# Fused sliding-window attention and gated MLP: first attention reordered with fewer fillers, zero fills and a value cast on GpSimd, second tile's attention later

## The chip, the cores and the metric

The kernel runs on one core of one Trainium2 chip. The metric is device time in microseconds (us), from repeated executions. Engine names in the profile: PE is TensorE (PEld its weight loads), DVE is VectorE, ACT is ScalarE, POOL is GpSimd, SP is SyncE. The clock is the share of its full speed that TensorE was granted.

## The reference

Attention over 8 batches of 8 heads, 576 positions, head size 64; heads 0 to 3 see the last 32 positions ("plain"), heads 4 to 7 every fourth of the last 128 ("dilated"). Its output is the input of a gated MLP.

```python
mask_plain = (rel >= 0) & (rel < 32)
mask_dil   = (rel >= 0) & (rel < 32 * 4) & (rel % 4 == 0)
scores = where(masks, (q @ k.T) / 8, -1e9)
attn   = softmax(scores) @ v                    # 8 x 8 x 576 x 64
x = attn.transpose(0, 2, 1, 3).reshape(4608, 512)
h = x @ w_in                                    # 4608 x 2048
g = h * sigmoid(beta * h)
out = g @ w_out                                 # 4608 x 512
```

## The kernel before

The 4608 tokens go through the MLP in nine tiles of 512. The attention of one batch is a list of short steps, and these are dealt out between the up-projection products ("slots") of the tile before. So in the first tile's MLP runs the second attention, in the second tile's MLP the third, and so on. Only the first attention runs with nothing to lie beside, and fillers keep TensorE running there. I call the fill of the pipeline up to the first tanh the start, and the stretch between the first tanh of a tile and that of the next the length of the tile.

In the lists, the first digit of a score, value or output step is the head pair: 0 and 1 are plain, 2 and 3 dilated.

```python
# W<n> n filler matmuls on a zero tile    K<x> Q<x> transposes of keys, queries, and their copies
# S<x><j> scores and exponential          V<x><j> value product and normalisation
# X<x><j> transposes of the output        H<n> first half of an up projection
# v0 v1 v2 casts of values (dilated, dilated, plain)   z0-z2 zero fills   q0-q3 query spreads
FIRST = (
    "W10 K2 W2 Q2 W2 K3 S20 S21 Q3 W2 S22 S23 S30 W1 S31 S32 W1 S33 v0 z0 W3 V20 V21 v1 W3 K0 W2 V22 K1 W3 V23 Q0 W2 "
    "V30 W2 V31 W2 X20 S00 V32 S01 V33 X21 S02 S10 X30 S11 V00 S12 X31 V01 H0 X00 V10 H1 X01 V11 X10 X11 "
    "z1 z2"
).split()
# ... SECOND cut
THIRD = (
    "S20 S21 S22 q0 S23 V20 S30 q1 V21 S31 q2 V22 S32 q3 V23 S33 V30 X20 S00 V31 "
    "S01 X21 V32 S02 V33 v2 S10 V00 X30 S11 V01 S12 X31 V10 X00 V11 X01 X10 X11"
).split()
# ... cut
    FROM = {1: 2}      # tile index 1 (the second): attention steps start at slot 2
# ... cut: the gate of one up-projection product; hps is its PSUM tile
        nc.scalar.activation(
            out=tnh[:], in_=hps, func=ACT.Tanh, scale=beta_half[:, fb:fb + 1])
        nc.vector.scalar_tensor_tensor(
            out=g[:], in0=tnh[:], scalar=1.0, in1=hps, op0=ALU.add, op1=ALU.mult)
# ... cut: a query spread of the third attention, on VectorE
        copy_on(eng)(
            out=qq[b % 2][64 * hf:64 * hf + 64, :, :, e],
            in_=raw[b, "q"][64 * e:64 * e + 64].rearrange("p (h i u) -> p h i u", h=4, i=NI))
# ... cut: who runs the steps that aren't matmuls
            eng = (nc.scalar if name[0] == "v" and (b, name) in ((2, "v2"),) else
                   nc.vector)
```

The tile `hps` lies in PSUM, the memory that this kernel's matmuls write. It is free for the next projection only when the gate product on VectorE has read it. Everything that stands before a gate product in VectorE's queue can so make TensorE wait.

The softmax here doesn't subtract the row's maximum and nothing guards it: scores larger than these inputs give would overflow.

## Time and profile before

| | before |
|---|---|
| median of 3 runs | 329.09 us (328.75 to 329.39) |
| span of the profiled execution | 327.5 us |
| first tanh of tiles 1, 2, 3 | 26.64, 63.38, 96.46 us |
| length of tile 1, 2, 3 | 36.74, 33.08, 30.15 us |
| TensorE clock, every stretch | 1.00 |

A line of the timeline has its start, its duration, the engine and the line of the kernel, the operation with output and input, and in brackets how long the engine was idle just before and what ended that. A line of the waits has the engine and line, what it waited for, the total, how often, and the longest.

### The profile page before, as it was taken

Reading aid. Unit: us, or ns where it says so; the run is one execution under the profiler, and the core shown is the slowest. Engines: PE = TensorE matmul, PEld = TensorE weight load, DVE = VectorE, ACT = ScalarE, POOL = GpSimd, SP = SyncE. Lnnn points to the kernel's source line nnn. Section 1 sums busy time; section 2 is a strip of 40 time slices with the busy share of each in tenths; the row PEclk is TensorE's granted clock in tenths of the full one; section 3 lists DMA queues with packets and bytes.
Section 4 is the critical chain, followed back from the end, with each engine's and each line's share of the span. In section 5 each row is a group of like instructions: output and inputs, shape, how many; then the busy total and the mean of one; then the engine's idle time right before and its main releaser. Section 6 shows DMA issues by size and latency. Waiting matters only on the chain.

```text
span 327.5 us, 6356 instructions
## 1 busy us (share of the span) xinstructions
PE 314.7 (96%) x2395; PEld 168.7 (52%) x2440; DVE 192.4 (59%) x432; ACT 195.6 (60%) x378; POOL 133.1 (41%) x174
## 2 busy tenths in 40 slices
PE   8999999998899999999999999999999999999995
PEld 3664565554555555555555555555555444444444
DVE  4668664787638883967396739673865344244400
ACT  3677774676666766666667666766666555355411
POOL 8943398362376266435643564355434000000000
PEclk9999999999999999999999999999999999999999
DMA  6999999999989798896869778872101210011131
GB/s 90 167 204 197 203 213 162 178 211 224 173 154 178 158 135 167 168 180 90 179 137 187 104 150 177 178 102 66 32 3 32 66 33 33 32 34 32 32 98 65
DMA packets 72223, 41.12 MB, mean 126 GB/s; under 512 B 55024, under 2 KB 67328, under 8 KB 71808
## 3 DMA queue, kind: packets, MB, share of 16 engines
q1 hardware_dynamic: 57264, 25.58, 41.7%
q0 software_dynamic: 14928, 15.14, 29.5%
q8 instruction: 19, 0.31, 0.4%
q14 instruction: 12, 0.10, 0.1%
HBM read 39.32 MB, written 16.52 MB: 170 GB/s over the span
## 4 chain that ended last, share of the span: by engine, by line
PE 90%; DVE 5%; ACT 3%; issue 2%; DVEq 0%; ACTq 0%
PE h_ps L514 32%; PE o_ps L552 28%; PE at L552 5%; PE at L452 4%; PE at L514 4%; PE o_ps L491 3%; PE at L469 3%; PE at L426 2%; PE at L419 2%; DVE g L524 2%; DVE xs L459 1%; ACT tnh L521 1%; PE at L571 1%; PE at L407 1%; PE at L355 1%
## 5 line engine op out<-in xcount | busy, mean ns | idle before, releaser
L524 DVE SCALAR_TENSOR_TENSOR g<-tnh,h_ps 128x512 bf16<-128x512 bf16 x130 | 88.9, 684 | 89.1 <-ACT tnh L521 88.4
L514 PE MATMUL h_ps<-xT,w_in_bf 128*128 128x512 bf16 x503 | 129.4, 379 | 3.0 <-DVE g L524 1.6
L521 ACT ACTIVATE tnh<-h_ps,beta_half 128x512 bf16<-128x512 f32 x130 | 89.4, 687 | 55.9 <-PE h_ps L514 53.3
L552 PE MATMUL o_ps<-w_out_bf,g 128*128 128x512 bf16 x443 | 113.6, 379 | 1.1
L514 PEld LDWEIGHTS <-w_in_bf 128*128 128x128 bf16 x576 | 51.7, 97 | 51.0 <-issue 2.9
L552 PEld LDWEIGHTS <-g 128*128 128x128 bf16 x560 | 50.4, 98 | 47.5
L432 ACT ACTIVATE pt<-at 128x384 bf16<-128x384 f32 (+2 forms) x107 | 46.1, 438 | 15.1 <-PE at L419 7.2
L434 POOL TENSOR_TENSOR pt<-pt,mask_d 96x384 bf16<-96x384 bf16 (+1 forms) x48 | 37.0, 781 | 41.0 <-ACT pt L432 40.3
L459 DVE TENSOR_TENSOR xs<-at,rcp 48x256 bf16<-48x256 f32 (+2 forms) x91 | 42.1, 463 | 8.5 <-PE at L469 4.3
L434 POOL TENSOR_TENSOR pt<-pt,mask_PP 128x384 bf16<-128x384 bf16 x24 | 22.7, 945 | 37.2 <-ACT pt L432 37.1
L452 PEld LDWEIGHTS <-pt 128*128 128x128 bf16 (+2 forms) x448 | 24.5, 97 | 15.8 <-issue 1.0
L560 ACT ACTIVATE osb<-o_ps 128x512 f32<-128x512 f32 x28 | 16.7, 597 | 19.0 <-PE o_ps L552 18.7
L455 DVE RECIPROCAL rcp<-at 48x4 f32<-48x4 f32 (+2 forms) x91 | 16.0, 176 | 7.1 <-PE at L452 6.3
L469 PEld LDWEIGHTS <-xs 96*128 96x128 bf16 (+1 forms) x224 | 13.5, 96 | 11.5 <-issue 2.6
L552 PE MATMUL at<-w_out_bf,g 128*128 128x512 bf16 x79 | 19.3, 379 | 0.1
L426 PEld LDWEIGHTS <-kdT 128*96 128x96 bf16 (+1 forms) x128 | 14.3, 120 | 9.8
L469 PE MATMUL at<-ident_b,xs 96*128 96x96 bf16 (+1 forms) x224 | 18.2, 199 | 0.7 <-ACT xT L475 0.5
L434 POOL TENSOR_TENSOR pt<-pt,mask_FP 128x384 bf16<-128x384 bf16 x12 | 10.9, 911 | 18.5 <-ACT pt L432 18.5
L452 PE MATMUL at<-vd,pt 96*128 96x65 bf16 (+1 forms) x244 | 17.4, 193 | 0.3 <-ACT qq L391 0.3
L426 PE MATMUL at<-qzd,kdT 128*80 128x96 bf16 (+1 forms) x122 | 17.1, 226 | 0.1
L483 ACT COPY xT<-at 128x384 bf16<-128x384 bf16 (+1 forms) x32 | 12.7, 396 | 4.9 <-PE at L469 4.9
L514 PE MATMUL at<-xT,w_in_bf 128*128 128x512 bf16 x54 | 13.6, 379 | 0.2
(116 smaller groups left out, 253.1 us busy)
## 6 DMA issues: line engine op xcount, KB each, us to landing
vp_st<-in_v_dram SPq DMA_DIRECT2D x12, 384.0 KB, 8.8
qk<-in_k_dram POOLq DMA_DIRECT2D x6, 576.0 KB, 6.6
qk<-in_q_dram POOLq DMA_DIRECT2D x6, 576.0 KB, 9.1
vd_st<-in_v_dram SPq DMA_DIRECT2D x6, 384.0 KB, 5.5
w_out_bf<-in_moe_w_out_dram POOLq DMA_DIRECT2D x4, 512.0 KB, 17.1
vd_st<-in_v_dram SPq DMA_DIRECT2D x6, 320.0 KB, 6.6
out_dram<-osb SPq DMA_DIRECT2D x7, 256.0 KB, 2.9
out_dram<-osb SPq DMA_DIRECT2D x8, 224.0 KB, 2.4
```

The source lines that it names most:

```text
L426: nc.tensor.matmul(sc[0:K, a, 0:2 * n], lhsT=kd[b][:, rp, h4, DO[hf]:DO[hf] + K], rhs=qzd[b % 2][:, :, rp, h4, hf * DQ[0]:hf * DQ[0] + n], ...
L432: nc.scalar.activation(out=w, in_=sc[0:K, :, 0:2 * n], func=ACT.Exp, scale=SCALE)
L434: nc.gpsimd.tensor_tensor(out=w, in0=w, in1=mask[0:K], op=ALU.mult)
L452: nc.tensor.matmul(pv[:, a, h2, :], lhsT=pt[x][0:K, c:c + P], rhs=rhs, start=True, stop=True)
L455: nc.vector.reciprocal(out=rcp[0:n, 0:m], in_=pv[0:n, :, :, D])
L459: nc.vector.tensor_tensor(out=xs_t[b, x, jx][:, a0:a0 + m], in0=pv[0:n, :, :, 0:D], in1=rcp[0:n, 0:m].unsqueeze(3).to_broadcast([n, m, 2, ...
L469: nc.tensor.transpose(xp[:, a * n:(a + 1) * n], xs[:, a].rearrange("p h d -> p (h d)"), ident_b[0:n, 0:n])
L514: nc.tensor.matmul(hps, lhsT=w_in_bf[:, kt, fb * P:(fb + 1) * P], rhs=xT[:, kt, t * NTOK:(t + 1) * NTOK], start=(kt == 2), stop=(kt == 1))
L521: nc.scalar.activation(out=tnh[:], in_=hps, func=ACT.Tanh, scale=beta_half[:, fb:fb + 1])
L524: nc.vector.scalar_tensor_tensor(out=g[:], in0=tnh[:], scalar=1.0, in1=hps, op0=ALU.add, op1=ALU.mult)
L552: nc.tensor.matmul(ops[:], lhsT=g_t[t, fb][:, tb * P:(tb + 1) * P], rhs=w_out_bf[:, fb, :], start=(fb == 0), stop=(fb == NFB - 1))
L560: nc.scalar.mul(out=osb[:], in_=ops[:], mul=0.5)
```

## The change

The intent: in the first attention, the zero fill `z0` comes first, casts of dilated values and first value products move in among the scores of the second pair, the plain scores come right after the plain query copies, and ten fillers stay where there were 21 (part a). The zero fills for the second attention go from VectorE to GpSimd (b). The third attention's cast of plain values goes from ScalarE to GpSimd, and is issued earlier, at step V23 in place of after V33 (c). The second tile's attention steps start two slots later (d).

```diff
 FIRST = (
-    "W10 K2 W2 Q2 W2 K3 S20 S21 Q3 W2 S22 S23 S30 W1 S31 S32 W1 S33 v0 z0 W3 V20 V21 v1 W3 K0 W2 V22 K1 W3 V23 Q0 W2 "
-    "V30 W2 V31 W2 X20 S00 V32 S01 V33 X21 S02 S10 X30 S11 V00 S12 X31 V01 H0 X00 V10 H1 X01 V11 X10 X11 "
-    "z1 z2"
+    "W10 K2 W2 Q2 W2 K3 z0 S20 S21 Q3 v0 v1 W1 S22 S23 S30 V20 W1 S31 V21 W1 S32 V22 S33 X20 W1 V23 W2 K0 W1 V30 K1 W1 Q0 W2 S00 V31 "
+    "S01 X21 V32 S02 V33 S10 X30 S11 V00 S12 X31 V01 H0 X00 V10 H1 X01 V11 X10 X11"
 ).split()
@@ THIRD
-    "S01 X21 V32 S02 V33 v2 S10 V00 X30 S11 V01 S12 X31 V10 X00 V11 X01 X10 X11"
+    "S01 X21 V32 S02 V33 S10 V00 X30 S11 V01 S12 X31 V10 X00 V11 X01 X10 X11"
@@
-    FROM = {1: 2}
+    FROM = {1: 4}
@@ extras
                 if b == 2:
+                    at("V23", cast_v, b, 2, G)
@@
     load_w_out(2)
+    zeros_q(1, 1, G)
+    zeros_q(1, 2, G)
     load_vp_1(1, G)
```

## The prediction

> **What bounds the kernel now.** I first read the page's busy shares, then the busy time of each engine in stretches of the span, to see where TensorE has room at all.
>
> ```profile
> PE 314.7 (96%) x2395; PEld 168.7 (52%) x2440; DVE 192.4 (59%) x432; ACT 195.6 (60%) x378; POOL 133.1 (41%) x174
> ...
> 60.00:70.00 10.00, 9.85 (x65) 5.12 (x63) 8.44 (x16) 7.69 (x17) 6.54 (x9) 1.00 1.07 200
> 70.00:80.00 10.00, 8.60 (x67) 4.59 (x67) 8.73 (x21) 6.28 (x13) 3.08 (x5) 1.00 1.21 221
> 80.00:100.00 20.00, 18.58 (x153) 10.15 (x155) 10.10 (x22) 13.36 (x27) 11.96 (x13) 1.00 1.00 170
> 100.00:150.00 50.00, 49.43 (x378) 26.47 (x384) 36.58 (x83) 33.58 (x66) 23.45 (x28) 1.00 0.92 164
> ```
>
> The columns of the stretches are the length, then busy time of TensorE, weight loads, VectorE, ScalarE and GpSimd, the granted clock, and two of DMA. From 100 us to 300 us TensorE is busy in 49.4 to 49.7 of every 50 us: nothing there can be gained by moving other engines' work, and the change doesn't touch it. Room lies in two places only: the first attention, before about 26 us (where part of the busy time is filler: matmuls of a zero tile that only keep the array running), and the second tile's stretch of 62 to 95 us, where 2 us slices add up to about 2.9 us of idle TensorE. What that idle waits for is in the view of waits on TensorE, longest first (the times are totals, count, longest):
>
> ```profile
> PE h_ps L514 <- DVE g L524: 1.6, 3, 0.8
> PE o_ps L491 <- DVE neg_d L162: 1.3, 1, 1.3
> PE at L452 <- ACT vp L334: 0.9, 1, 0.9
> PE at L469 <- ACT xT L475: 0.5, 1, 0.5
> ```
>
> The second is the start. The first and third are in the second tile: the up projection waits for a PSUM buffer that VectorE has yet to read, and the value product waits for a float32 to bf16 cast on ScalarE. In the timeline that cast is one instruction, and GpSimd does the same one in the later tiles in the same time:
>
> ```profile
> 85.49 1.46 ACT L334 CAST vp<-vp_st 128x1536 bf16<-128x1536 f32 x1
> ...
> 87.01 0.34 PE L452 MATMUL at<-vp,pt 128*128 128x65 bf16 x6 [0.89 <-ACT vp L334]
> ...
> 93.06 1.46 POOL L334 CAST vp<-vp_st 128x1536 bf16<-128x1536 f32 x1
> ```
>
> For the first attention I took the timeline of 8 to 27 us and wrote down when the plain heads' transposes, the query copies and the first plain scores run (L413 is the plain score product):
>
> ```profile
> 13.17 0.65 PE L367 MATMUL h_ps<-ident_b,xT 64*64 64x64 bf16 x18
> 13.61 0.72 DVE L338 COPY vd<-vp_st 80x1024 bf16<-80x1024 bf16 x1
> 16.07 1.02 PE L367 MATMUL at<-ident_b,xT 64*64 64x64 bf16 x36
> 17.12 1.83 ACT L391 COPY qq<-at 64x576 bf16<-64x576 bf16 x3 [1.19 <-PE at L367]
> 18.91 0.33 PE L413 MATMUL h_ps<-qq,xT 128*128 128x192 bf16 x2
> 18.95 0.48 ACT L483 COPY xT<-at 128x384 bf16<-128x384 bf16 x1
> 19.32 0.50 ACT L432 ACTIVATE pt<-h_ps 128x384 bf16<-128x384 f32 x1
> ```
>
> The plain queries' transposes start at 16.07 us, although their DMA, issued at 7.34 us and 7.4 us to landing by the view of DMA issues, is in at 14.8 us. The first plain exponential starts at 19.32 us, behind three query copies and one copy of the attention output, all on ScalarE. From there ScalarE works on without a gap to 22.7 us, and the last attention matmul that the up projection needs comes 6.9 us after it, at 26.23 us.
>
> **What the Trainium skill says.** "VectorE: DVE Perf Modes", section "Zero memsets can be issued as uint32", says a memset costs a cycle per element whatever the type. The trace agrees in shape: VectorE fills 64x576 uint32 in 0.54 us, and GpSimd fills 64x1536 bf16 in 1.38 us, so the same bytes cost GpSimd about twice as long. "SBUF — State Buffer", section "Who interferes with whom", says a VectorE copy in a two-port mode and a GpSimd instruction exclude each other for a whole instruction. The four query spreads of the second tile took 1.04, 0.46, 0.67 and 0.46 us; the slow two lie beside GpSimd's mask products, so it agrees. "PSUM — Partial Sum Buffer", section "PSUM bank collisions raise a hardware error", tells to guard a bank against two engines' reads; this kernel's query copies do it: at 9.96 us VectorE's second copy waits 0.23 us for ScalarE's copy of the same bank. "TensorE: Matmul & The Clock Gate", section "What's actually happening", says that an idle window of about 3.4 us halves the clock. The trace has clock 1.00 in every stretch to 300 us, with the fillers in place.
>
> **The change part by part.**
>
> (a) First attention. In program order eleven filler matmuls go (21 stood after the opening fourteen; ten stay). A filler that runs while TensorE would wait anyway costs nothing, so 11 x 0.215 us = 2.4 us (0.215 us is the pitch at which these matmuls start) is an upper bound, not the gain. I walk the new order by hand with the old durations. VectorE now clears the query buffer (two fills, pitch 0.70 us) before, not after, it copies the second pair's queries: that copy moves from 9.27 us to about 9.9 us, ends 10.3 us, and ScalarE's copy of the same bank, which must follow it, moves from 9.83 us to 10.4 us. Scores of the second pair so start about 0.5 us later. The two casts of dilated values follow on VectorE at 10.6 us and 11.25 us (their second DMA lands near 11.2 us); the second takes 0.4 to 0.7 us. So the first value product runs at 11.1 us instead of 11.97 us, but VectorE's first normalisation only after the second cast, at 12.0 us; two of them at 0.6 us each let the output transposes run at about 13.2 us. After these TensorE still has one filler, a value product (0.12 us), two fillers, the key transposes (0.58), a filler, a value product, 0.58 us, a filler: 2.7 us, so the plain queries' transposes start at about 15.9 us against 16.07 us. Nearly nothing is won there. What is won: the copy of attention output (0.37 us from its start to the next) has left the queue between the query copies and the first exponential. ScalarE reaches that exponential at about 18.8 us instead of 19.32 us. The tail from there on has the same instructions in almost the same order, so the up projection starts about 0.5 us earlier. I give this part 0.5 us, with 0 to 1 us possible.
>
> (b) The zero fills of the second attention leave VectorE, where they ran from 25.27 to 27.90 us: four of 0.54 us. The first gate product waits for them about 0.5 us (27.83 against 27.33 us, when its tanh ends). But TensorE doesn't: the 48 up-projection, 8 down-projection matmuls and 48 transposes between 26.23 and 40.12 us come to 56 x 0.215 + 4 x 0.4 = 13.6 us of 13.9 us. Gain 0 to 0.2 us. On GpSimd they become four fills of 1152 elements, by the ratio above about 1.04 us each, 4.2 us in all, starting near 30.45 us. They push the following DMA issue from 31.77 us to about 34.7 us and the next from 34.85 us to 36.1 us. These transfers take 14 to 16 us from issue to landing, behind a full queue (about 200 GB/s), so a later issue shortens the queue rather than delays the landing. Cost 0.
>
> (c) The value cast of the third attention moves from ScalarE to GpSimd, which has idle of 3.6 us just there. That removes the wait of 0.89 us and nothing else is due at that point: the masked scores it needs were done at 82.5 us. Gain 0.9 us.
>
> (d) The second tile's attention starts two up-projection slots later, and the slot arithmetic makes up for it by the end. The steps that hurt stay together: each of the last query spreads and a normalisation stand before a gate product while only two PSUM buffers hold projections. Walking the new queue (gate product 0.70, spread 0.55, normalisation 0.6, slot 0.86 us), I get about 1.0 us of waits in place of 1.3 us at the two worst places, but the moved cast may hold the shared ports against the last spread for up to 0.45 us. Gain 0.3 us, within -0.3 to 0.6 us.
>
> Sum: 0.5 + 0.1 + 0.9 + 0.3 = 1.8 us, so 329.09 - 1.8 = 327.3 us.
>
> **The rivals.** First, the fillers are truly on the path: in the chain that ended last the filler line holds 10% of the first 100 us. Ten microseconds of fillers in the chain, less the opening, would make all 2.4 us of (a) count and the time 325.4 us; for it speaks that the plain queries have landed 1.25 us before use. Against it, VectorE's two early casts and fills stand in the way of exactly those steps. Second, the first attention gets slower: the second cast waits for its DMA at the head of VectorE's queue, and if that lands later or GpSimd's descriptor work blocks the copy, everything behind waits; 1 us lost there gives 328.8 us. Third, the PE clock drops with fewer fillers: I see no wait over 0.6 us, so I hold it for unlikely; it would cost several us. Fourth, the second tile's later attention only moves the VectorE pile-up into slots with fewer PSUM buffers and gives back the 0.9 us: 328.2 us. Fifth, GpSimd's fills make it late for the dilated value casts at 40.68 us; but it waited 2.40 us there for the DMA, which isn't delayed, so no.
>
> **Range and chances.** The parts' spreads (about 0.5 us for (a), 0.4 us for (c) and (d) together, 0.2 us of run scatter) give 326.1 to 328.7 us for 8 in 10. Being over 2% faster means under 322.5 us, more than all idle that I found in the two places; slower by 2% needs the clock or a blocked queue. Hence 0.03, 0.95, 0.02.
>
> **What would show it.** Right: no wait on a ScalarE value cast; the up projection's first tanh near 26.1 us instead of 26.64 us; the plain query transposes still near 16 us; TensorE waits for gate products of about 1 us between 70 and 80 us; stretches after 100 us unchanged. Wrong: query transposes near 15 us (first rival), a long VectorE wait on the value DMA near 11 us, a clock under 1.00 before 30 us, or a new wait on GpSimd between 74 and 90 us.

## More of the kernel before

All runs here were classed fast.

From 60 to 100 us TensorE is busy 37.03 us (the sum of its three stretches there), so idle for 3 us.

## The result, and the profile after

The changed kernel took 327.69 us (median of four runs, 327.18 to 328.24), the kernel before 329.24 us (328.75 to 329.50) in the same rounds. The ratio is 0.9955, 95% interval 0.9935 to 0.9976. A ratio here is the mean time of one kernel's fast runs over that of the other's of the same rounds, so not quite the ratio of the medians quoted. A second set of five runs, e12 below, gave 0.9949. The change gains 1.6 us, clear of noise and well under 2%, as the prediction's chances (faster by over 2%, neither, slower by over 2%) had it.

Where it gains is seen best in the first tanh of each tile, from the two timelines:

| | before | after | difference |
|---|---|---|---|
| first tanh of tile 1 | 26.64 | 26.09 | -0.55 |
| length of tile 1 | 36.74 | 36.75 | +0.01 |
| length of tile 2 | 33.08 | 31.81 | -1.27 |
| first tanh of tile 3 | 96.46 | 94.65 | -1.81 |
| span | 327.5 | 325.9 | -1.6 |

The first tanh before and after:

```profile
26.64 0.69 ACT L521 ACTIVATE tnh<-h_ps,beta_half 128x512 bf16<-128x512 f32 x1 [0.47 <-PE h_ps L514]
...
26.09 0.69 ACT L520 ACTIVATE tnh<-h_ps,beta_half 128x512 bf16<-128x512 f32 x1 [0.46 <-PE h_ps L513]
```

In these two traces the start gave about a third and the second tile the rest. About 0.2 us is lost again in a later tile (33.29 us in place of 33.08 us for the fifth), which the diff doesn't touch. All five traces with the new order of the first attention as the change has it (after, e2, e6, e7, e12) show this loss, and none of the other nine does. Since e2 has part (a) alone, it goes with (a), whose net worth in this trace is so about 0.35 us. Why it arises is not shown.

The page's busy line of the changed kernel, then its stretches (length; busy time of PE, PEld, DVE, ACT, POOL; clock; two of DMA):

```profile
PE 312.7 (96%) x2384; PEld 167.3 (51%) x2429; DVE 190.2 (58%) x428; ACT 194.9 (60%) x377; POOL 138.3 (42%) x179
```

```profile
60.00:70.00 10.00, 9.85 (x60) 4.96 (x60) 7.43 (x14) 7.89 (x16) 6.11 (x9) 1.00 1.18 209
70.00:80.00 10.00, 8.90 (x69) 4.82 (x69) 8.51 (x21) 6.35 (x13) 5.41 (x6) 1.00 1.09 205
80.00:100.00 20.00, 19.23 (x161) 10.55 (x163) 12.09 (x27) 12.78 (x27) 11.95 (x13) 1.00 1.02 178
100.00:150.00 50.00, 49.44 (x382) 26.49 (x388) 36.70 (x84) 33.39 (x65) 23.43 (x27) 1.00 0.96 164
```

TensorE has eleven matmuls fewer (2384 against 2395: the fillers). From 60 to 100 us it is busy 37.98 us where it was 37.03 us, so 0.95 us of idle have gone there. From 100 to 150 us it is busy for the same time (49.44 against 49.43 us). The waits of TensorE, longest total first:

```profile
PE h_ps L513 <- DVE g L523: 1.6, 3, 0.6
PE o_ps L490 <- DVE neg_d L161: 1.3, 1, 1.3
PE at L412 <- ACT qq L390: 0.6, 1, 0.6
PE at L468 <- ACT xT L474: 0.5, 1, 0.5
```

(Lines are numbered one lower than before: L513 was L514.) The wait of 0.9 us for the value cast is gone. The waits for gate products (`g`) still sum to 1.6 us. The two between 70 and 80 us fell from 0.84 and 0.47 us to 0.45 and 0.59 us, as predicted (about 1.0 us in place of 1.3 us), but a third, at 80.6 us, is 0.51 us where one of 0.27 us was. The timeline shows where the moved cast came to lie:

```profile
74.02 0.45 DVE L302 COPY qq<-qpT 64x1152 bf16<-64x1152 bf16 x1
74.04 1.02 PE L513 MATMUL h_ps<-xT,w_in_bf 128*128 128x512 bf16 x3 [0.45 <-DVE g L523]
...
75.02 1.46 POOL L333 CAST vp<-vp_st 128x1536 bf16<-128x1536 f32 x1
75.06 1.45 DVE L523 SCALAR_TENSOR_TENSOR g<-tnh,h_ps 128x512 bf16<-128x512 bf16 x2
75.78 1.02 PE L513 MATMUL h_ps<-xT,w_in_bf 128*128 128x512 bf16 x4 [0.59 <-DVE g L523]
76.54 0.46 DVE L302 COPY qq<-qpT 64x1152 bf16<-64x1152 bf16 x1
```

The cast ends at 76.48 us, between two query spreads that take 0.45 and 0.46 us. Beside it run two gate products, of 0.67 and 0.69 us (the merged line has the gap between them too), as long as the same pair takes in e4, where no cast runs beside it. So this cast holds up nothing, and whether that is luck is the question of the experiments. In the start, the same view shows

```profile
16.01 0.56 PE L366 MATMUL h_ps<-ident_b,xT 64*64 64x64 bf16 x15
...
18.29 0.33 PE L412 MATMUL at<-qq,xT 128*128 128x192 bf16 x2 [0.56 <-ACT qq L390]
...
18.80 0.86 ACT L431 ACTIVATE pt<-at 128x384 bf16<-128x384 f32 x2
```

The plain query transposes start at 16.01 us (16.07 before), and the first plain exponential at 18.80 us (19.32 before).

One caution: the start varies between executions. Three traces with the same first attention and the same fills (after, e7, e12) have the first tanh at 26.09, 25.67 and 26.26 us, and the five traces with the first attention of the kernel before (before, e1, e3, e4, e9) have it anywhere from 26.23 to 27.30 us. Differences of the start below a microsecond can't be read from one pair of traces.

### The profile page after: what moved, and what is told of

Same layout as the page of the kernel before. It is cut to its first block, busy times and chain, and to the rows that moved or that the text cites. A ratio compares the mean times of both kernels' runs of the same rounds, so it can differ in the third digit from the quotient of the medians.

```text
span 325.9 us, 6336 instructions
## 1 busy us (share of the span) xinstructions
PE 312.7 (96%) x2384; PEld 167.3 (51%) x2429; DVE 190.2 (58%) x428; ACT 194.9 (60%) x377; POOL 138.3 (42%) x179
## 4 chain that ended last, share of the span: by engine, by line
PE 87%; DVE 5%; ACT 2%; DMA 2%; issue 2%; POOL 1%; DVEq 0%; POOLq 0%; ACTq 0%
PE h_ps L513 33%; PE o_ps L551 29%; PE at L551 5%; PE at L451 4%; PE at L513 4%; PE at L468 3%; PE at L418 2%; DMA vp_st<-in_v_dram 2%; PE at L425 2%; DVE g L523 2%; DVE xs L458 2%; PE at L570 1%; ACT tnh L520 1%; PE h_ps L551 1%; PE at L406 1%
## 5 line engine op out<-in xcount | busy, mean ns | idle before, releaser
L513 PE MATMUL h_ps<-xT,w_in_bf 128*128 128x512 bf16 x503 | 129.2, 379 | 2.9 <-DVE g L523 1.6
L513 PEld LDWEIGHTS <-w_in_bf 128*128 128x128 bf16 x576 | 51.8, 97 | 51.5 <-issue 3.2
L451 PE MATMUL at<-vd,pt 80*128 80x65 bf16 (+1 forms) x244 | 17.4, 193 | 0.5 <-ACT qq L390 0.3
L513 PE MATMUL at<-xT,w_in_bf 128*128 128x512 bf16 x53 | 13.5, 379 | 0.2
```

The lines of the kernel that those rows point to most:

```text
L451: nc.tensor.matmul(pv[:, a, h2, :], lhsT=pt[x][0:K, c:c + P], rhs=rhs, start=True, stop=True)
L513: nc.tensor.matmul(hps, lhsT=w_in_bf[:, kt, fb * P:(fb + 1) * P], rhs=xT[:, kt, t * NTOK:(t + 1) * NTOK], start=(kt == 2), stop=(kt == 1))
```

## The experiments

Each kernel had five rounds, and the kernel before ran beside it on the same chip: 329.28 us for e1 to e4, 329.44 us for e5 to e8, 329.37 us for e9 to e12 (medians of 11 runs each). My theory after the result was the prediction's: four parts that add up. The rivals were that one part carries everything, or that parts need each other. All kernels gave correct results.

### e1_cast: part (c) alone

```diff
-    "S01 X21 V32 S02 V33 v2 S10 V00 ...
+    "S01 X21 V32 S02 V33 S10 V00 ...
@@ extras, b == 2
+                    at("V23", cast_v, b, 2, G)
```

> The kernel before with part (c) alone: the value cast of the third attention on GpSimd instead of ScalarE, all else as before. My theory: TensorE's wait of 0.9 us for that cast goes and nothing replaces it, so the second tile is 0.9 to 1.1 us shorter (from its first tanh at 63.4 us to the third tile's at 96.46 us: 33.1 us before, 32.1 us expected), the first tanh stays at 26.6 us, total -0.9 us. Rival: GpSimd's cast holds the shared ports against VectorE's last query spread and gives the gain back in waits for gate products: total 0 to -0.4 us.

Measured: 330.91 us, ratio 1.0030 (0.9992 to 1.0068). The gain of 0.9 us didn't come. The six runs fall in two groups: 328.18 and 328.44 us, at a mean clock of 0.998, and 330.73 to 331.90 us, four runs all at 0.995. The profiled execution, which is the first of the six, is of the second group. Its second tile takes 34.52 us. Timeline and stretches:

```profile
73.63 2.07 DVE L303 COPY qq<-qpT 64x1152 bf16<-64x1152 bf16 x1
...
73.93 1.47 POOL L334 CAST vp<-vp_st 128x1536 bf16<-128x1536 f32 x1
...
77.01 3.36 PE L514 MATMUL h_ps<-xT,w_in_bf 128*128 128x512 bf16 x8 [2.25 <-DVE g L524]
```

```profile
74.00:76.00 2.00, 0.71 (x5) 0.35 (x4) 1.93 (x3) 1.13 (x3) 1.70 (x2) 1.00 1.08 200
76.00:78.00 2.00, 0.99 (x3) 0.41 (x3) 1.94 (x6) 0.00 (x0) 0.23 (x1) 0.65 1.06 199
78.00:80.00 2.00, 2.00 (x7) 0.66 (x5) 0.94 (x2) 0.69 (x1) 0.00 (x0) 0.50 0.95 160
```

A query spread that takes 0.46 us alone takes 2.07 us here: it ends 0.30 us after the cast. The gate product behind it is late by as much, and TensorE waits 2.25 us, to 77.01 us. Towards the end of that wait, at 76.6 us, its clock falls to half, and it stays there to 80.0 us (the means are 0.65 and 0.50 in the two stretches shown). The two fast runs say what (c) is worth when the clock holds: about 1 us gained (328.3 against 329.28 us). They have no trace, so this rests on their recorded clocks alone.

### e2_first and e3_fills: parts (a) and (b) alone

e2 has the new order with ten fillers and keeps `z1 z2` at its end, on VectorE. e3 has the old order and only moves the fills:

```diff
-    "z1 z2"
@@
     load_w_out(2)
+    zeros_q(1, 1, G)
+    zeros_q(1, 2, G)
```

> The kernel before with the new order of the first attention alone; the second attention's zero fills stay on VectorE at its end. My theory: first tanh at 26.1 us instead of 26.64 us, total -0.5 us, and the fills, still there, cost TensorE nothing. Rival: part of the changed kernel's early gain came from the fills leaving VectorE; then the first tanh is later than 26.3 us or the second tile starts less than 0.4 us earlier (tanh at 63.4 us before).

> The kernel before with the zero fills alone moved from VectorE to GpSimd. My theory: first gate product 0.5 us earlier, TensorE unchanged; the second tile's first tanh stays at 63.4 us within 0.15 us, total 0 (-0.2 to +0.2 us). Rival A: VectorE's relief reaches TensorE: -0.4 us or more. Rival B: the later DMA issues on GpSimd delay landings: +0.3 us or more.

Measured: e2 329.14 us, ratio 0.9998 (0.9987 to 1.0010); e3 329.22 us, ratio 0.9995 (0.9983 to 1.0007). Neither differs from before. In e2's trace the first tanh comes at 26.20 us, in e3's at 26.70 us (before 26.64), and the second tile takes 33.08 and 33.06 us. So e2 shows the earlier start in the trace but only 0.1 us in the time, less than the scatter of the start. Its trace also loses 0.2 us in the fifth tile, so that its span is only 0.2 us shorter than before.

### e4_late: part (d) alone

```diff
-    FROM = {1: 2}
+    FROM = {1: 4}
```

> The kernel before with part (d) alone: the second tile's attention starts two up-projection slots later. My theory after seeing the changed kernel's trace, where waits for gate products stayed at 1.6 us: the pile-up on VectorE only moves; second tile 0 to 0.3 us shorter, total 0 to -0.3 us. Rival: it removes the pile-up and the cast's wait overlaps with it, so that alone it gives -0.6 us or more.

Measured: 329.14 us, ratio 0.9997 (0.9986 to 1.0009). In the trace the second tile takes 32.79 us, 0.29 us less than before, and the waits for gate products sum to 1.4 us (1.6 before); the wait for the value cast grew from 0.9 to 1.1 us, so these two together don't account for the 0.29 us. Its start was late (first tanh 27.30 us), which hides the 0.29 us in that execution.

So far the parts alone, by medians: -0.1 (a), -0.1 (b), +1.6 (c) and -0.1 us (d). That is +1.3 us, where the whole change gives -1.6 us. The parts don't add up. The traces suggest that (c) and (d) are the two that meet; e7 tests it.

### e7_no_late: the changed kernel without (d)

```diff
-    FROM = {1: 4}
+    FROM = {1: 2}
```

> The changed kernel with part (d) undone: the second tile's attention starts after two slots again. My theory: within 0.3 us of the changed kernel. Rival: (d) is needed for the cast on GpSimd to pay: the second tile is 0.5 us or more longer than the changed kernel's 31.8 us.

Measured: 329.84 us, ratio 1.0011 (0.9988 to 1.0033), runs from 328.35 to 331.07 us, three of six at clock 0.995. In the trace the second tile takes 35.36 us in place of 31.81 us. The waits for gate products sum to 2.8 us, the longest 1.5 us: again a spread (1.37 us) lies beside the cast.

```profile
74.50 1.46 POOL L333 CAST vp<-vp_st 128x1536 bf16<-128x1536 f32 x1 [1.19 <-DMA vp_st<-in_v_dram]
74.91 1.37 DVE L302 COPY qq<-qpT 64x1152 bf16<-64x1152 bf16 x1
```

Here too the clock is at half for 3.4 us, from 77.9 us on. The three runs whose clock held took 328.35, 328.82 and 329.83 us. Taking (d) away costs about 2 us (329.84 against the 327.69 and 327.77 us of the changed kernel in other batches; by the ratios 0.6% of 329 us), although alone it gives 0.1 us. That is the interaction. (No run has (c) and (d) without the rest.)

### e9_cast_later: part (c) alone, after the last spread

If the collision does the harm, a cast placed elsewhere needs no (d).

```diff
 # the kernel before, with v2 out of THIRD
@@ extras, b == 2
+                    at("V30", cast_v, b, 2, G)
```

> The kernel before with one thing changed: the cast of the second pair's values runs on GpSimd after the last query spread of that pair (three score-value steps further on than in the changed kernel), the second tile's attention starting as before. If the collision with a query spread is what made the cast alone cost time, this cast meets none: the wait of 0.9 us for the cast is gone, the second tile takes about 32.1 us from first tanh to first tanh (33.1 before), no clock drop, time 0.9 to 1.1 us below before (ratio about 0.997), all runs alike. Rival: the cast on GpSimd hurts wherever it stands unless the second tile's attention starts later; then second tile 33.5 us or more, runs spread over 2 us and more, ratio 1.000 or above.

Measured: 328.67 us, ratio 0.9975 (0.9963 to 0.9987), all five runs between 328.05 and 328.71 us. The second tile takes 32.40 us (expected 32.1).

```profile
75.09 0.45 DVE L303 COPY qq<-qpT 64x1152 bf16<-64x1152 bf16 x1
...
75.90 1.45 POOL L334 CAST vp<-vp_st 128x1536 bf16<-128x1536 f32 x1
76.01 0.67 DVE L524 SCALAR_TENSOR_TENSOR g<-tnh,h_ps 128x512 bf16<-128x512 bf16 x1
```

The last spread is done before the cast begins, and the gate product beside it takes its usual 0.67 us. The same cast, on the same engine, moved two steps on in the list (from V23 past S33 to V30; the expectation counts three), turns a loss of 1.6 us into a gain of 0.7 us. The theory of the collision holds. The gain is 0.2 us short because waits for gate products are 1.9 us here, 0.3 more than before: -0.89 + 0.3 comes near the -0.68 us measured in the tile. The two longest (0.84 and 0.60 us) are for gate products that stand in VectorE's queue behind spreads and normalisations.

### e5_old_few and e10_old_few_all: order or fillers?

e5 is the kernel before with eleven fillers fewer and nothing else; e10 is the changed kernel with that list (without `z1 z2`):

```diff
-    "... S20 S21 Q3 W2 S22 S23 S30 W1 S31 S32 W1 S33 v0 z0 W3 V20 V21 v1 W3 K0 W2 V22 K1 W3 V23 Q0 W2 "
-    "V30 W2 V31 W2 X20 ...
+    "... S20 S21 Q3 W1 S22 S23 S30 W1 S31 S32 S33 v0 z0 W2 V20 V21 v1 W1 K0 W1 V22 K1 W1 V23 Q0 W1 "
+    "V30 W1 V31 W1 X20 ...
```

> The kernel before, old order of the first attention, but with eleven filler matmuls fewer (as many as the changed kernel drops), nothing else. My theory: fillers mostly cover waits for VectorE, ScalarE and DMA, yet some stand before the plain query transposes; these move from 16.07 us to about 15.5 us and the first tanh from 26.64 us to about 26.2 us; total -0.3 to -0.5 us. Rival 1 (fillers truly on the path): -2 us or more. Rival 2 (fillers free): 0. Rival 3 (they hold the clock up): slower, clock under 1.00.

> The changed kernel with the first attention in the old order, but with the fillers as few as the new order has. If what the first attention gained came from fewer fillers and not from the order, this is as fast as the changed kernel or a little faster: last plain query transposes at about 15.2 us (16.0 in the changed kernel), first tanh at 25.5 to 26, ratio 0.993 to 0.996. Rival: the order itself is worth something (copy of the attention outputs out of ScalarE's way before the first plain exponential): then slower than the changed kernel by 0.3 to 0.5 us, ratio 0.997, first tanh at 26.6.

Measured: e5 328.93 us, ratio 0.9991 (0.9978 to 1.0004); e10 327.34 us, ratio 0.9944 (0.9932 to 0.9956), against 0.9949 for the changed kernel beside it. The plain query transposes start at 15.16 us (e5) and 15.61 us (e10), the first plain exponential at 18.32 and 18.77 us, the first tanh at 25.54 and 25.99 us. From e10:

```profile
15.61 1.02 PE L366 MATMUL at<-ident_b,xT 64*64 64x64 bf16 x36
...
18.77 0.49 ACT L431 ACTIVATE pt<-h_ps 128x384 bf16<-128x384 f32 x1
```

With as many fillers, the old order is as good as the new one. The new order wins at ScalarE: from the start of these transposes to the exponential it needs 2.79 us, the old one 3.16 us. It loses that again by transposes that start later, and by the 0.2 us in the fifth tile, which e10 doesn't have. The times of e2 and e5 alone are within noise of the kernel before, so the gain of the start is best seen in all traces: the first tanh is at 26.23 to 27.30 us (mean 26.7) in the five with the old order and 21 fillers, at 25.54 and 25.99 us in the two with the old order and ten, and at 25.67 to 26.26 us (mean 26.1) in the four with the new order and ten. So what (a) brings comes from the eleven fillers. The new order with all 21 was not run, so what the order is worth beside them stays open.

### e6_new_none: the changed kernel without further fillers

```diff
-    "... Q3 v0 v1 W1 S22 S23 S30 V20 W1 S31 V21 W1 S32 V22 S33 X20 W1 V23 W2 K0 W1 V30 K1 W1 Q0 W2 S00 V31 "
+    "... Q3 v0 v1 S22 S23 S30 V20 S31 V21 S32 V22 S33 X20 V23 K0 V30 K1 Q0 S00 V31 "
```

> The changed kernel with the ten fillers that it kept after the opening fourteen also removed. My theory: five of them stand between the output transposes at 13.1 us and the plain query transposes, 1.1 us, of which the landing of the queries and the copies let about 0.8 us through: query transposes near 15.2 us, first tanh near 25.4 us, total -0.6 us against the changed kernel. Rival: the clock falls in the first 30 us (under 1.00) and the time rises by 1 us or more.

Measured: 329.66 us, ratio 0.9987 (0.9960 to 1.0014), five of six runs at 328.80 to 329.77 us with a mean clock of 0.984 to 0.989, one at 326.46 us with clock 1.000. In the trace the query transposes start at 14.97 us, near the expected 15.2, but then

```profile
14.00:16.00 2.00, 1.90 (x61) 1.69 (x60) 1.08 (x4) 1.28 (x2) 1.43 (x4) 1.00 2.33 144
16.00:18.00 2.00, 1.04 (x8) 0.66 (x9) 0.42 (x2) 1.94 (x4) 2.00 (x4) 0.53 1.47 191
18.00:20.00 2.00, 2.00 (x19) 1.38 (x18) 1.18 (x4) 1.09 (x4) 0.82 (x2) 0.50 1.29 205
```

with this line of the timeline,

```profile
17.26 0.48 PE L412 MATMUL at<-qq,xT 128*128 128x192 bf16 x2 [0.96 <-ACT qq L390]
```

and the first tanh comes at 27.29 us. The longest TensorE wait between 8 and 32 us is this one of 0.96 us, and it didn't bring the clock down: it began at 16.3 us, and a mean clock of 0.53 from 16 to 18 us means that the fall to half came at about 16.1 us. From 12.6 us to there no wait is over 0.3 us. From 12 to 16 us the profile has TensorE busy for 3.53 us, and for 3.55 us in the changed kernel, which keeps its clock. So neither a long wait nor a low busy share marks the fall here; what e6 lacks are the fillers. The ten fillers that the change keeps do work: without them the clock falls in most runs and costs some 3 us; in the run where it holds, the kernel is 1.2 us faster than the changed one (326.46 against 327.7 us).

### e8_keys_early and e11_keys_spreads: towards a better version

e8 is the changed kernel with the plain keys transposed before the attention output, and one of ScalarE's three plain query copies on VectorE. Six of the ten fillers stay (its expectation counts three fewer, but it is four). It changes three things at once, and no run here separates them.

```diff
-    "... V20 W1 S31 V21 W1 S32 V22 S33 X20 W1 V23 W2 K0 W1 V30 K1 W1 Q0 W2 S00 V31 "
+    "... V20 W1 S31 V21 S32 V22 S33 W1 K0 X20 V23 W1 K1 V30 W1 Q0 W1 S00 V31 "
@@
-            copy_on(nc.scalar if hf or b == 0 and x == 0 and n else nc.vector)(
+            copy_on(nc.scalar if hf else nc.vector)(
```

e11 is e8 with earlier query spreads in the third attention, and its cast after the last one:

```diff
-    "S20 S21 S22 q0 S23 V20 S30 q1 V21 S31 q2 V22 S32 q3 V23 S33 V30 X20 S00 V31 "
+    "q0 S20 S21 q1 S22 S23 V20 S30 V21 S31 q2 V22 S32 q3 V23 S33 V30 X20 S00 V31 "
@@
-                    at("V23", cast_v, b, 2, G)
+                    at("V30", cast_v, b, 2, G)
```

> The changed kernel with the plain key transposes placed before the first output transposes, three fillers fewer and one of ScalarE's three query copies given to VectorE, which idled 1.3 us there. My theory: the changed kernel's early gain is limited by the plain query transposes at 16.0 us and by ScalarE's three copies after them; here the transposes start near 15.0 us (their DMA lands at 14.8 us), the first plain exponential near 17.5 us instead of 18.8 us, the first tanh near 25.0 us; total -1.0 us against the changed kernel. Rival: the tail after the first scores is what binds, and the first tanh stays above 25.8 us.

> The kernel with keys first (the best so far, ratio 0.992) with the third pair's query spreads each one step earlier and the value cast after the last of them. If the spreads in VectorE's queue ahead of gate products are what still makes TensorE wait in the second tile (waits for gate products 1.6 us in three), those waits fall to about 1.0 us and the time to about 326.2 us (ratio 0.9905). Rival: the waits only move to other gate products, or the spreads meet the zero fills or other GpSimd work: waits 1.5 us or more and the ratio 0.992 or above.

Measured: e8 326.63 us (326.02 to 327.64), ratio 0.9918 (0.9903 to 0.9932): transposes at 14.98 us, exponential at 17.63 us, first tanh at 25.06 us, second tile 31.81 us, clock 0.997 or more in every run. It beats both kernels, by about 2.7 and 1.0 us. e11 326.61 us, ratio 0.9916 (0.9900 to 0.9932): no better than e8. From 60 to 98 us its waits for gate products are 1.5 us, as in e8, and its second tile takes 31.79 us. The rival was right: the waits only moved. Six of e11's runs took 325.88 to 327.31 us; the profiled one took 329.76 us, mainly because the first weights of the down projection landed late:

```profile
37.05 1.02 PE L551 MATMUL o_ps<-w_out_bf,g 128*128 128x512 bf16 x4 [2.25 <-DMA w_out_bf<-in_moe_w_out_dram]
```

No other trace shows that wait. Its first tile is 3.0 us and its third 1.0 us longer than elsewhere, so the second tile's length was read from a disturbed execution. Whether the earlier start makes it likelier, one run of seven can't tell.

### e12_again: the changed kernel again

Unchanged code, as the yardstick of the last batch.

> The changed kernel once more, on the chip of these runs, as the yardstick for the other three: ratio 0.9955 within 0.002, all runs within 1.2 us of each other. If it ranges over more than 2 us here, as the kernels with the cast and no late start did, its own gain is not steady.

Measured: 327.77 us (327.00 to 327.89), ratio 0.9949 (0.9937 to 0.9961). The cast starts at 75.17 us, ends at 76.63 us, and the next spread starts at 76.71 us. The gap of 0.08 us was 0.06 us in the first trace. It repeats, and the nine runs of this kernel have none with the slow group's clock. In both traces the spread is also behind two gate products in VectorE's queue that take as long as the cast. The second tile takes 31.82 us.

## Why the prediction was right, and where it was wrong

The time and its range held: 327.3 us predicted, 327.69 us measured. By pairs, the sum of 1.8 us held too: (a) and (b) predicted 0.6 us, seen 0.4 to 0.55 us as an earlier first tanh in the two traces, whose scatter is larger, less the 0.2 us in the fifth tile; (c) and (d) predicted 1.2 us, seen 1.27 us. The steps inside were partly wrong, and that the sum of (c) and (d) came out was in part luck, as below.

**(a), right in what the trace would show, wrong in the cause.** The transposes stayed at 16 us and the exponential came at 18.8 us, as worked out by hand. (What the prediction calls the last attention matmul, at 26.23 us, is the up projection's first one after the last output copy; nothing rests on it.) But the prediction gave the 0.5 us to the order, and held the fillers for an upper bound that mostly costs nothing. e10 shows the reverse: with as few fillers the old order does as well (0.9944 against 0.9949). The failed term is the one taken for nearly nothing, the eleven fillers. The first rival, that all 2.4 us of them are on the path, fell as well: in e5 and e10 the first tanh is 1.2 and 0.7 us before the mean of the five traces with all fillers, and e5 gains 0.5 us in the median.

**(b), right.** e3 moves the time by -0.06 us, the predicted 0 to 0.2. The fills took 1.05 to 1.06 us each on GpSimd, as estimated.

**(c), the step that failed: "That removes the wait of 0.89 us and nothing else is due at that point".** The wait did go. But something was due: a query spread on VectorE. Alone (e1), the cast stretched it to 2.07 us, made TensorE wait 2.25 us and in four of six runs dropped the clock. The prediction saw that "the moved cast may hold the shared ports against the last spread for up to 0.45 us", and put it under (d) as a small deduction. It was mis-sized: the copy became 0.9 us (e7) to 1.6 us (e1) longer, and in both traces the clock then fell to half for 3.4 us.

**(d), right in size alone, incomplete in reason.** Alone it saves 0.29 us in the trace, the predicted 0.3. At the two places that the prediction walked through, the waits for gate products fell as it said, from 1.31 to 1.04 us, in e4 and in the changed kernel alike; but in the changed kernel a third wait grew, so that all of them still sum to 1.6 us. With (c) it is worth about 2 us (e7), since it shifts VectorE's queue so that the cast falls between two spreads. That the sum came out rests on this gap, which the prediction hadn't worked out: the next spread starts 0.06 us after the cast's end. That was luck.

**Rivals.** The third, the clock, was dismissed as unlikely because no wait was over 0.6 us. The dismissal was right for this change, whose runs all keep the clock, but the reason was not: in e6, with ten fillers less, the clock falls though the longest wait between 8 us and the fall is 0.7 us, and there is none over 0.3 us in the last 3.4 us. The fourth, a VectorE pile-up that gives back the 0.9 us, happened without (d), not with it. The second showed as a wait of 0.49 us of VectorE for the second value load, at 11.43 us, with no slower start; the fifth did not come.

**Still open.** Of the start's 0.4 us in e2's trace, 0.2 us is lost again in the fifth tile; the rest of the difference to the 0.1 us in its time is below the scatter of the start. No trace was taken of e1's fast group, so it isn't shown whether the cast and the spread meet there. The 0.2 us lost in the fifth tile goes with the new order (five traces of five, none of nine) and has no cause here.

## What to carry to other kernels

Moving work to an idle engine isn't priced by the wait it removes alone: ask which instruction of the other engine it will lie beside, and try it at several points of the schedule (here +1.6 us or -0.7 us, two steps apart). Parts of a change should be measured both alone and left out, because a part that is worth nothing alone (0.1 us) can be what makes another pay (about 2 us). Fillers that keep the clock are worth counting: too many stand on the path, too few let the clock fall, and a spread of several runs with their clocks shows on which side one is.

## What the Trainium skill lacked or had wrong

- "TensorE: Matmul & The Clock Gate", section "What's actually happening", gives an idle window of about 3.4 us as the condition for half clock. The length fits: the clock was at half for 3.4 us in e1 and e7, and for 6.8 us, twice that, in e6. But "idle" can't mean that no matmul runs: in e1 the clock fell after 1.8 us of a wait of 2.25 us, and in e6 after 3.4 us without a wait over 0.3 us. The page tells elsewhere, under "A second HAM failure mode: psum-queue depth-cycling", of frequent short idling that does it; neither place says what share of a window counts as idle. That only some executions are hit (four of six, five of six) fits the free-running window that the section describes; no run here tests it.
- "SBUF — State Buffer", section "Who interferes with whom", agrees in the main: the copy ends only after the cast (2.07 us in place of 0.46), and a gate product with one SBUF input is not slowed (0.67 and 0.69 us beside the cast). But it says that whoever issues first gets the shared ports. In e1's trace the copy starts at 73.63 us, while a mask product runs on GpSimd to 73.99 us, and the cast at 73.93 us, yet the cast ends first, at 75.39 us, and the copy at 75.71 us. It is one case, and the spans of GpSimd in a profile are rough.
- None of the pages that I used has the duration of a GpSimd zero fill: 64x1152 bf16 took 1.05 to 1.06 us, while VectorE clears 64x576 uint32, the same bytes, in 0.54 us.
- None of them has how much such a start varies: the same first attention had its first tanh at 26.23 to 27.30 us in five traces.
